# An attention block and a feed-forward block in one kernel: from a scheduler's order over four segments to a written order over eight chunks

## The chip, the core and the metric

The kernel runs on one core of a Trainium2 chip. The core has TensorE (PE: matrix products, written to PSUM), VectorE (DVE), ScalarE (ACT: exponentials, gelu, copies), GpSimd (POOL) and SyncE (SP, which here only issues transfers). The metric is device time in microseconds (us) of one execution. Each engine works through its own list of instructions in order and waits on semaphores for the others. In the profile "PEld" is the loading of the stationary operand of a product.

## The reference

Inputs are bf16; x is 2048 tokens of 576 numbers, with 32 heads of 18 numbers each.

```python
h  = x + A(layernorm(x))          # attention
h2 = h + B(layernorm(h))          # feed-forward

def A(x):                          # 4 segments of 512 tokens, M = z = 0
    q, k, v = x @ wq, x @ wk, x @ wv                 # 32 heads of 18
    for s in range(4):
        p     = softmax(q_s k_s^T * 18**-0.5, causal mask)
        a_dot = p @ v_s
        a_mem = (phi(q_s) @ M) / (phi(q_s) @ z + 1e-6)   # phi(t) = t+1 if t>0 else exp(t)
        o     = g * a_mem + (1 - g) * a_dot              # g = sigmoid(beta), per head
        M    += phi(k_s)^T v_s ;  z += sum(phi(k_s))
    return o @ wo
def B(x):
    return gelu(x @ w1 + b1) @ w2 + b2                   # 576 -> 4608 -> 576
```

The attention works inside a segment of 512 tokens; from one segment to the next only M and z go on. The feed-forward block works on each token alone.

## The kernel before, in words

Work is cut by segment of 512 tokens, four tiles of 128 tokens each. `phase_P(s)` (L218) projects: for each tile it takes the layernorm, turns it (L195), multiplies by wq, wk and wv in two halves of 288 columns (`proj`, L203 and L205), copies q and k into padded tiles (L72), turns them per group of four heads (L259, L264) and adds phi(k)^T v to M and z (L281 to L288). `load_w` fetches these weights again in every segment.

`phase_A(s)` (L300) goes over eight groups of four heads. For each group it has three steps: keys 0 to 127; keys 128 to 255 together with 384 to 511; keys 256 to 383. A step's scores (L338) are products over 32 rows, the four heads at four positions of the array. They go to two PSUM units of two banks, two heads in each, and each unit has its own exponential (L347). POOL then masks the diagonal blocks (L349), and the products with v (L356), 19 columns wide, add into one bank `ox`. That bank is cleared by DVE (L308), also holds the memory part (L323) and is read by DVE at the end of a group (L361 to L371).

`phase_B(s)` (L378) turns the result, multiplies by wo, adds x (L392), takes the second layernorm, and turns that into `xn2T_s`. It stores h + b2 to memory (`hd`, L402).

`phase_C(s)` (L405) is the feed-forward block on 512 tokens. The first layer takes w1 in nine groups of 512 columns. A group's weights `w1g` come in by three transfers on SP's queue (L410, L413, L414) into one of two buffers, are used for four blocks of five products of 512 columns (L419, L420), and DVE copies each block to `hT` (L424). After every three groups one gelu over 6144 numbers per partition runs in place (L428). The second layer (L437) is, for each tile and half, 36 products of 288 columns, added up in one bank; DVE adds `hc` (h + b2, read back, L432) and the result is stored (L441). w2 (5.3 MB) stays on the core; it is loaded once (L169), behind the first segment's inputs.

The source calls P, A and B for all segments and then C for all, but that is not the order in which the engines work. A scheduling layer places the instructions of all engines by priority, with the scores at a higher one (L334), so that products of the feed-forward block stand between the attention's products from the second segment on.

Of the kernel before, what the change touches and what calls it, by code (L numbers as in the profile page):

```python
# [16 lines left out]
def kernel(  # L17
# [15 lines left out]
    dbg = None  # L33
    nseg_run = None
# [6 lines left out]
    L = 512  # L41
    NSEG = S // L
    TPS = L // P
# [6 lines left out]
    XW = 640  # L50
    scale = float(Dh) ** -0.5
    EPS = 1e-5
    BIG = 3.0e38
    GB = 3
    FORCE4 = False
    HIPRI = True
    GB = 3
    EVAC_ACT = 0
    XT_DVE = False
    QK_DVE = False  # L60

    def copy_xt(out, in_):
        if XT_DVE:
            nc.vector.tensor_copy(out=out, in_=in_)
        else:
            nc.scalar.copy(out=out, in_=in_)  # L66

    def copy_qk(out, in_):
        if QK_DVE:
            nc.vector.tensor_copy(out=out, in_=in_)  # L70
        else:
            nc.scalar.copy(out=out, in_=in_)  # L72
    if nseg_run is None:
        nseg_run = NSEG
# [3 lines left out]
    wpool = ctx.enter_context(tc.tile_pool(name="wpool", bufs=1))  # L78
    xpool = ctx.enter_context(tc.tile_pool(name="xpool", bufs=2))
    xtp = ctx.enter_context(tc.tile_pool(name="xtp", bufs=2))  # L80
    xn2Tp = ctx.enter_context(tc.tile_pool(name="xn2Tp", bufs=2))
    tmp1 = ctx.enter_context(tc.tile_pool(name="tmp1", bufs=1))
    alpool = ctx.enter_context(tc.tile_pool(name="alpool", bufs=1))
    ptpool = ctx.enter_context(tc.tile_pool(name="ptpool", bufs=2))
    ptpool1 = ctx.enter_context(tc.tile_pool(name="ptpool1", bufs=1))
    hpool = ctx.enter_context(tc.tile_pool(name="hpool", bufs=2))
    hbpool = ctx.enter_context(tc.tile_pool(name="hbpool", bufs=1))
# [3 lines left out]
    psS = ctx.enter_context(tc.tile_pool(name="psS", bufs=2, space=PSUM))  # L91
# [3 lines left out]
    x_pre = []  # L95
    for tl in range(TPS):
        xt = xpool.tile([P, D], BF16, tag="x", name="xt") if tl < 2 else None
        if xt is not None:
            nc.sync.dma_start(out=xt[:], in_=x[tl * P:(tl + 1) * P, :])
        x_pre.append(xt)  # L100

    def load_w(W, tag):
        wt = wpool.tile([P, KT, D], BF16, tag=tag, name="wt_" + tag)
        nc.sync.dma_start(out=wt[:, 0:4, :], in_=W[0:512, :].rearrange("(k p) n -> p k n", p=P))
        nc.sync.dma_start(out=wt[0:64, 4, :], in_=W[512:576, :])
        nc.gpsimd.memset(wt[64:KTAIL, 4, :], 0.0)
        return wt

    w_pre = {"wq": load_w(A_wq, "wq"), "wk": load_w(A_wk, "wk"), "wvo": load_w(A_wv, "wvo")}
# [3 lines left out]
    maskcol = const.tile([P, 1], F32, name="maskcol")  # L113
    nc.vector.memset(maskcol[:], 0.0)
    for i in range(4):
        nc.vector.memset(maskcol[32 * i:32 * i + Dh, :], 1.0)
# [3 lines left out]
    beta_bc = const.tile([P, H], BF16, name="beta_bc")  # L120
    nc.sync.dma_start(out=beta_bc[:], in_=A_beta.partition_broadcast(P))
    g_bc = const.tile([P, H], F32, name="g_bc")
    nc.scalar.activation(out=g_bc[:], in_=beta_bc[:], func=ACT.Sigmoid)
    omg_bc = const.tile([P, H], F32, name="omg_bc")
    nc.vector.tensor_scalar(out=omg_bc[:], in0=g_bc[:], scalar1=-1.0, scalar2=1.0, op0=ALU.mult, op1=ALU.add)
    gmzm = const.tile([P, G, Dh], F32, name="gmzm")
    for i in range(4):
        src = g_bc[32 * i:32 * i + 32, :].rearrange("p (g i) -> p g i", i=4)[:, :, i:i + 1]
        nc.vector.tensor_scalar(out=gmzm[32 * i:32 * i + 32, :, :], in0=src.to_broadcast([32, G, Dh]),
                                scalar1=maskcol[32 * i:32 * i + 32, :], scalar2=None, op0=ALU.mult)  # L130

    b2_bc = const.tile([P, D], BF16, name="b2_bc")
    nc.sync.dma_start(out=b2_bc[:], in_=B_b2.partition_broadcast(P))
    b1_row = B_b1.rearrange("(o f) -> o f", o=1)
# [6 lines left out]
    q_pads = [const.tile([P, H, 32], BF16, name=f"q_pad{j}") for j in range(2)]  # L141
    k_pads = [const.tile([P, H, 32], BF16, name=f"k_pad{j}") for j in range(2)]
    phik_pads = [const.tile([P, H, 32], BF16, name=f"phik_pad{j}") for j in range(TPS)]
    v_augs = [const.tile([P, H, Dh + 1], BF16, name=f"v_aug{j}") for j in range(TPS)]
    xn_bufs = [const.tile([P, XW], BF16, name=f"xn{j}") for j in range(2)]
    xn2_bufs = [const.tile([P, XW], BF16, name=f"xn2_{j}") for j in range(1)]
    o_nat = const.tile([P, TPS, XW], BF16, name="o_nat")
    for tx in xn_bufs:
        nc.gpsimd.memset(tx[:, D:XW], 0.0)
    for tpad in q_pads + k_pads:  # L150
        nc.gpsimd.memset(tpad[:, :, Dh:32], 0.0)
    for tpad in phik_pads:
        nc.vector.memset(tpad[:, :, Dh:32], 0.0)
    for tv in v_augs:
        nc.vector.memset(tv[:, :, Dh:Dh + 1], 1.0)
    for tx in xn2_bufs:
        nc.gpsimd.memset(tx[:, D:XW], 0.0)
        nc.gpsimd.memset(tx[:, D:D + 1], 1.0)
    nc.gpsimd.memset(o_nat[:, :, D:XW], 0.0)

    hd = tc.dram_tile([S, D], F32, name="hd")
    hT = const.tile([P, NF, L], BF16, name="hT")
    w2_sb = const.tile([P, NF, D], BF16, name="w2_sb")
    w2v = B_w2.rearrange("(f p) d -> p f d", p=P)
    late = {"x_last": None, "w2_last": None}

    def issue_w2():
        for c in range(4):
            d = nc.sync.dma_start(out=w2_sb[:, c * 9:(c + 1) * 9, :], in_=w2v[:, c * 9:(c + 1) * 9, :])  # L169
            if late["x_last"] is not None:  # L170
                tc.add_manual_dep(d.ins, late["x_last"].ins.name, SYNC_DEP, reason="bulk FFN weights after the first segment's inputs")
            late["w2_last"] = d

    def layernorm(src, xn):
        stats = small.tile([P, 2, 6], F32, tag="stats", name="stats")
        for c in range(2):
            nc.vector.bn_stats(out=stats[:, c, :], in_=src[:, c * HALF:(c + 1) * HALF])  # L177
        mv = small.tile([P, 2], F32, tag="mv", name="mv")
        nc.vector.bn_aggr(out=mv[:], in_=stats[:])
        rstd = small.tile([P, 1], F32, tag="rstd", name="rstd")  # L180
        nc.vector.tensor_scalar(out=rstd[:], in0=mv[:, 1:2], scalar1=EPS, scalar2=None, op0=ALU.add)  # L181
        nc.gpsimd.tensor_tensor(out=rstd[:], in0=rstd[:], in1=mhalf[:], op=ALU.pow)  # L182
        nc.vector.tensor_scalar(out=xn[:, 0:D], in0=src, scalar1=mv[:, 0:1], scalar2=rstd[:],  # L183
                                op0=ALU.subtract, op1=ALU.mult)

    def unit2():
        return psS.tile([P, 2, 512], F32, tag="st2", name="u2")

    def bf16v(bank_ap):
        return bank_ap.bitcast(BF16)  # L190

    def transposes5(src, bank_ap):
        pt = bf16v(bank_ap)[:, 0:KT * P].rearrange("p (k q) -> p k q", q=P)
        for k in range(KT):
            nc.tensor.transpose(out=pt[:, k, :], in_=src[:, k * P:(k + 1) * P], identity=ident[:])  # L195
        return pt

    def proj(xT_t, wt):
        u = unit2()
        for hf in range(2):  # L200
            ps = u[:, hf, :]
            for k in range(4):
                nc.tensor.matmul(out=ps[:, 0:HALF], lhsT=xT_t[:, k, :], rhs=wt[:, k, hf * HALF:(hf + 1) * HALF],  # L203
                                 start=(k == 0), stop=False)
            nc.tensor.matmul(out=ps[:, 0:HALF], lhsT=xT_t[0:KTAIL, 4, :], rhs=wt[0:KTAIL, 4, hf * HALF:(hf + 1) * HALF],  # L205
                             start=False, stop=True)
        return u

    def hview(u):
        return u[:, :, 0:HALF].rearrange("p b (h d) -> p b h d", d=Dh)  # L210

    def pad_view(tpad):
        return tpad[:, :, 0:Dh].rearrange("p (b h) d -> p b h d", b=2)

    st_P = {}
    st_B = {}

    def phase_P(s):  # L218
        if s == 0:
            wq_t, wk_t, wv_t = w_pre["wq"], w_pre["wk"], w_pre["wvo"]  # L220
        else:
            wq_t = load_w(A_wq, "wq")
            wk_t = load_w(A_wk, "wk")
            wv_t = load_w(A_wv, "wvo")
        QT_al_s = alpool.tile([P, G, L], BF16, tag="qt", name="QT_al_s")
        KT_al_s = alpool.tile([P, G, L], BF16, tag="kt", name="KT_al_s")
        for tl in range(TPS):
            t = s * TPS + tl
            cols = slice(tl * P, (tl + 1) * P)
            if s == 0 and x_pre[tl] is not None:  # L230
                xt = x_pre[tl]
            else:
                xt = xpool.tile([P, D], BF16, tag="x", name="xt")
                xd = nc.sync.dma_start(out=xt[:], in_=x[t * P:(t + 1) * P, :])
                if s == 0:
                    late["x_last"] = xd
                    if tl == TPS - 1:
                        issue_w2()
# [259 lines left out]
```

## Time and profile before

| | |
|---|---|
| median of 3 runs | 618.51 us (617.55 to 622.82) |
| the profiled execution: span | 618.1 us |
| busy: PE / PEld / DVE / ACT / POOL | 553.5 / 331.1 / 327.6 / 319.4 / 154.1 us |
| first product, last product | 6.2 us, 614.6 us |
| first scores (L338), first product of the feed-forward block (L419) | 42.3 us, 119.7 us |
| TensorE's granted clock | half from about 47.9 to 123 us, full after that |
| transfers | 54.65 MB, 87 GB/s read and written over the span |
| gelu | 12 calls of 5.32 us; 17 loads of function tables of 1.28 us on ACT |

The profiled execution's own time is its span, 618.1 us, with nothing left out around it. PE's busy time is made of products that overlap one another, so what a product costs is read from the distance between the starts of two that follow each other, not from its own length.

### The profile page before, as it was taken

Reading aid. Unit: us, or ns where it says so; the run is one execution under the profiler, and the core shown is the slowest. Engines: PE = TensorE matmul, PEld = TensorE weight load, DVE = VectorE, ACT = ScalarE, POOL = GpSimd, SP = SyncE. Lnnn points to the kernel's source line nnn. Section 1 sums busy time; section 2 is a strip of 40 time slices with the busy share of each in tenths; the row PEclk is TensorE's granted clock in tenths of the full one; section 3 lists DMA queues with packets and bytes.
Section 4 is the critical chain, followed back from the end, with each engine's and each line's share of the span. In section 5 each row is a group of like instructions: output and inputs, shape, how many; then the busy total and the mean of one; then the engine's idle time right before and its main releaser. Section 6 shows DMA issues by size and latency. Waiting matters only on the chain. (4 is left out here: it accounts for less than half of the span.)

```text
span 618.1 us, 12146 instructions
## 1 busy us (share of the span) xinstructions
PE 553.5 (90%) x4992; PEld 331.1 (54%) x4992; DVE 327.6 (53%) x811; ACT 319.4 (52%) x342; POOL 154.1 (25%) x247
## 2 busy tenths in 40 slices
PE   2778875599999998999999998899999999999997
PEld 1553333375444566675444466665544567744576
DVE  5443223467777635647786735555687641166310
ACT  1449951134999931338788742368767540024300
POOL 3124432313342223224323123135331210000000
PEclk9995555599999999999999999999999999999999
DMA  7960003325223113322132333111124432144020
GB/s 194 351 201 3 2 1 97 110 65 147 65 79 110 45 59 123 104 75 85 43 89 67 114 117 117 58 45 30 31 78 116 109 123 77 38 135 129 25 58 20
DMA packets 48223, 54.65 MB, mean 88 GB/s; under 512 B 3204, under 2 KB 44072, under 8 KB 48168
## 3 DMA queue, kind: packets, MB, share of 16 engines
q1 hardware_dynamic: 48168, 53.88, 29.3%
q8 instruction: 39, 0.64, 0.4%
q14 instruction: 16, 0.13, 0.1%
HBM read 46.79 MB, written 7.08 MB: 87 GB/s over the span
## 5 line engine op out<-in xcount | busy, mean ns | idle before, releaser
L437 PEld LDWEIGHTS <-hT 128*128 128x128 bf16 x1152 | 107.5, 98 | 30.3 <-issue 3.5
L428 ACT ACTIVATE hT<-hT 128x6144 bf16<-128x6144 bf16 x12 | 63.9, 5324 | 55.8 <-DVE hT L424 55.7
L419 PEld LDWEIGHTS <-w1g 128*128 128x128 bf16 x576 | 51.3, 98 | 56.0 <-issue 7.4
L203 PEld LDWEIGHTS <-xnT_t 128*128 128x128 bf16 x384 | 36.7, 100 | 24.3 <-ACT xnT_t L66 13.4
L338 PEld LDWEIGHTS <-KT_al_s 32*128 32x128 bf16 x512 | 21.0, 93 | 50.9 <-issue 47.9
L401 POOL TENSOR_TENSOR hb<-h_t,b_bc 128x576 f32<-128x576 f32 x16 | 20.4, 1277 | 76.2 <-DVE h_t L392 76.2
L182 POOL TENSOR_TENSOR rstd<-rstd,mhalf 128x1 f32<-128x1 f32 x32 | 17.5, 549 | 40.3 <-DVE rstd L181 40.3
L314 POOL TENSOR_SCALAR r_g<-QT_al_s 128x512 bf16<-128x512 bf16 x24 | 14.7, 612 | 36.1 <-DVE pq L316 33.4
L420 PEld LDWEIGHTS <-w1g 65*128 65x128 bf16 x144 | 14.0, 97 | 14.4 <-issue 0.6
L312 ACT ACTIVATE e_g<-QT_al_s 128x512 bf16<-128x512 bf16 x24 | 15.1, 630 | 11.4 <-DVE pq L316 8.0
L203 PEld LDWEIGHTS <-oT_t 128*128 128x128 bf16 x128 | 13.6, 109 | 11.0 <-issue 4.2
L316 DVE SCALAR_TENSOR_TENSOR pq<-e_g,r_g 128x512 bf16<-128x512 bf16 x24 | 19.2, 801 | 0.3
L195 PEld LDWEIGHTS <-xn_0_167 128*128 128x128 bf16 x80 | 5.2, 107 | 22.5 <-DVE xn_0_167 L183 21.6
L308 DVE MEMSET ox<- 128x456 f32 x32 | 14.0, 438 | 3.6 <-DVE o_nat L365 1.4
L177 DVE BATCH_NORM_STATS2 stats<-xt 128x6 f32<-128x288 bf16 x32 | 13.5, 441 | 3.9 <-DMA xt<-in_A_x_dram 3.8
L183 DVE TENSOR_SCALAR xn_0_167<-h_t,mv,rstd 128x576 bf16<-128x576 f32 x16 | 9.3, 579 | 9.9 <-POOL rstd L182 9.9
L323 PEld LDWEIGHTS <-pq 128*128 128x128 bf16 x96 | 8.1, 97 | 11.9 <-issue 5.6
L177 DVE BATCH_NORM_STATS2 stats<-h_t 128x6 f32<-128x288 f32 x32 | 13.1, 451 | 0.4
L270 POOL TENSOR_SCALAR rk<-k_pad_155 128x576 bf16<-128x576 bf16 x8 | 5.4, 678 | 28.0 <-ACT k_pad_155 L72 28.0
L205 PEld LDWEIGHTS <-xnT_t 65*128 65x128 bf16 x96 | 9.7, 101 | 2.8
L270 POOL TENSOR_SCALAR rk<-k_pad_156 128x576 bf16<-128x576 bf16 x8 | 5.3, 666 | 21.9 <-ACT k_pad_156 L72 21.2
L428 ACT ACT_TABLE_LOAD x8 | 10.3, 1283 | 0.1
(1911 smaller groups left out, 1416.8 us busy)
## 6 DMA issues: line engine op xcount, KB each, us to landing
w1g<-in_B_w_dram SPq DMA_DIRECT2D x36, 512.0 KB
w_sb<-in_B_w_dram SPq DMA_DIRECT2D x4, 1296.0 KB
hd<-hb SPq DMA_DIRECT2D x16, 288.0 KB
hc<-hd SPq DMA_DIRECT2D x16, 288.0 KB
xt<-in_A_x_dram SPq DMA_DIRECT2D x16, 144.0 KB
wt_wq<-in_A_wq_dram SPq DMA_DIRECT2D x4, 576.0 KB
wt_wk<-in_A_wk_dram SPq DMA_DIRECT2D x4, 576.0 KB
wt_wvo<-in_A_wv_dram SPq DMA_DIRECT2D x4, 576.0 KB
```

Of the source, the lines that this page charges most:

```text
L177: nc.vector.bn_stats(out=stats[:, c, :], in_=src[:, c * HALF:(c + 1) * HALF])
L182: nc.gpsimd.tensor_tensor(out=rstd[:], in0=rstd[:], in1=mhalf[:], op=ALU.pow)
L203: nc.tensor.matmul(out=ps[:, 0:HALF], lhsT=xT_t[:, k, :], rhs=wt[:, k, hf * HALF:(hf + 1) * HALF], start=(k == 0), stop=False)
L308: nc.vector.memset(ox[:, 0:456], 0.0)
L312: nc.scalar.activation(out=e_g[:], in_=QT_al_s[:, g, :], func=ACT.Exp)
L314: nc.gpsimd.tensor_scalar(out=r_g[:], in0=QT_al_s[:, g, :], scalar1=BIG, scalar2=0.0, op0=ALU.min, op1=ALU.max)
L316: nc.vector.scalar_tensor_tensor(out=pq[:], in0=e_g[:], scalar=1.0, in1=r_g[:], op0=ALU.min, op1=ALU.add)
L338: mm = nc.tensor.matmul(out=sts[i // 2][:, i % 2, off:off + n], lhsT=KT_al_s[rows, g, kt * P:(kt + 1) * P], rhs=QT_al_s[rows, g, kt * P:L] ...
L401: nc.gpsimd.tensor_tensor(out=hb[:], in0=h_t[:], in1=b2_bc[:], op=ALU.add)
L419: nc.tensor.matmul(out=ps[:], lhsT=w1g[:, k, j * P:(j + 1) * P], rhs=xn2T_s[:, k, :], start=(k == 0), stop=False)
L428: nc.scalar.activation(out=hT[:, f0:f1, :], in_=hT[:, f0:f1, :], func=ACT.Gelu_apprx_tanh)
L437: nc.tensor.matmul(out=ps[:, 0:HALF], lhsT=hT[:, f, tl * P:(tl + 1) * P], rhs=w2_sb[:, f, hf * HALF:(hf + 1) * HALF], start=(f == 0), stop ...
```

## The change

The whole body is written anew. What is computed is the same.

- The work is cut into eight chunks of 256 tokens. Five generators give out the products: the second part of the attention for even and odd tiles (`stream_B`), the scores and what follows them (`stream_A`), the projections (`stream_P`) and the feed-forward block (`stream_F`).
- The order of PE's instructions is fixed in the source. A loop holds a clock `free["PE"]` and lists of taken spans for ACT, DVE and POOL, filled with durations written in the source (`pe(...)`, `op(...)`). It always goes on with the first generator, in the order B, A, P, F, whose inputs are ready by that table. The other engines' order is still the scheduling layer's.
- Scores go to one tile of four banks, all four heads at once, with one exponential per visit: 1536 numbers per partition where a visit has 384 columns, 2048 where it has 512. There is one such tile. An even chunk has one visit for each group of heads, an odd chunk two.
- Three single banks serve all the other products. Pairs of groups share a bank `ox`.
- The projections are four products of 432 columns over q, k and v together, whose weights are loaded once and stay. wo stays as well.
- The feed-forward block works on 256 tokens: a first-layer product is 256 columns wide, two blocks share a bank, gelu runs twice for each chunk (4608 numbers each), and the first half of the next chunk's first layer may stand ahead of this chunk's second layer. `w1g` still has two buffers, and w1 is fetched once for each chunk.
- w2 comes in six parts, after the fourth group of w1 has landed.

```diff
-    for s in range(n): phase_P(s); phase_A(s); phase_B(s)
-    for s in range(n): phase_C(s)
+    w1pool = ctx.enter_context(tc.tile_pool(name="w1pool", bufs=2))
+    psS = ctx.enter_context(tc.tile_pool(name="psS", bufs=1, space=PSUM))
+    psX = ctx.enter_context(tc.tile_pool(name="psX", bufs=1, space=PSUM))
+    psC = ctx.enter_context(tc.tile_pool(name="psC", bufs=3, space=PSUM))
+    def op(eng, dur, *deps):              # earliest free span of that engine
+        at = max(deps, default=0.0) + READ
+        ...
+    def pe(dur, *deps):
+        free["PE"] = max(free["PE"], max(deps, default=0.0)) + dur
+        return free["PE"] + DRAIN - READ
+    def load_w2(after):
+        for c in range(6):
+            d = nc.sync.dma_start(out=w2_sb[:, c * 6:(c + 1) * 6, :], in_=w2v[:, c * 6:(c + 1) * 6, :])
+            tc.add_manual_dep(d.ins, after.ins.name, SYNC_DEP, reason="FFN2 weights after the first FFN1 weights")
...
+        def scores(c, g, pieces):         # in stream_A: one visit
+            st = banks4()
+            for kt in pieces:
+                ...
+                for i in range(4):
+                    nc.tensor.matmul(out=st[:, i, off:off + n], lhsT=KTs[s0 + kt // 2][rows, g, (kt % 2) * P:(kt % 2 + 1) * P],
+                                     rhs=QTs[c][rows, g, lo * P:Q], start=True, stop=True, tile_position=(32 * i, 0))
+            r = pe(0.21 + off * MM / 1000, done_P[c])
+            nc.scalar.activation(out=pt_[:, :, 0:off], in_=st[:, :, 0:off], func=ACT.Exp, scale=scale)
+            lkS.give(op("ACT", 0.18 + 4 * off * 0.00083, r))
+            ...                           # masks of the diagonal blocks on POOL
...
+            plan = [[0, 1]] if half == 0 else [[0, 1], [2, 3]]
...
+    def ffn1(c, half):
+        for jp in range(9 * half, 9 * half + 9):
+            f = 2 * jp
+            ...                           # a new w1g where f % 4 == 0: L571 to L573
+                    if c == 0 and fg == W2_AFTER:   # W2_AFTER = 3
+                        load_w2(d)
+            yield lkC, done_B[c]
+            for a in range(2):
+                mm5(ps[:, a, :], lambda r, k: w1g[r, k, fs], lambda r, k: xn2T[r, k, :])
+            nc.vector.tensor_copy(out=hT[:, f:f + 2, :], in_=ps)
+        nc.scalar.activation(out=hv, in_=hv, func=ACT.Gelu_apprx_tanh)     # 18 blocks
...
+    def stream_F():
+        for c in range(NCH):
+            yield (lambda: c in done_B), 0.0
+            if ahead < c:
+                yield from ffn1(c, 0)
+            yield from ffn1(c, 1)
+            if c + 1 < NCH and c + 1 in done_B and done_B[c + 1] <= free["PE"]:
+                yield from ffn1(c + 1, 0)
+                ahead = c + 1
+            yield from ffn2(c)
+    streams = [stream_B(0), stream_B(1), stream_A(), stream_P(), stream_F()]
+    with tc.manual_schedule(engines={mybir.EngineType.PE}):
+        ...
+            pick = next((g for g, at in live if at <= t0 + 0.02), None)
+            if pick is None:
+                pick = min(live, key=lambda e: e[1])[0]
+            waits[pick] = next(pick)
```

## The prediction

> **What bounds the kernel now.** The page's busy times come first, then the stretches by window, then the timeline of PE. Everything is set against the profiled execution's own 618.1 us; the three runs' median, 618.51, is the same within 0.1%.
>
> ```profile
> span 618.1 us, 12146 instructions
> PE 553.5 (90%) x4992; PEld 331.1 (54%) x4992; DVE 327.6 (53%) x811; ACT 319.4 (52%) x342; POOL 154.1 (25%) x247
> PEclk9995555599999999999999999999999999999999
> ```
>
> PE is the bound on average, but its clock was halved for five of forty slices. By window (length; busy of PE, PEld, DVE, ACT, POOL; clock; transfer share; GB/s), cut where the first scores, the first feed-forward product and the last attention end:
>
> ```profile
> 0.00:42.30 42.30, 23.69 (x207) 17.96 (x208) 19.85 (x58) 12.88 (x19) 10.46 (x28) 1.00 0.81 245
> 42.30:119.70 77.40, 52.66 (x564) 27.54 (x563) 25.82 (x72) 45.64 (x56) 28.44 (x43) 0.54 0.18 55
> 119.70:500.00 380.30, 364.56 (x3447) 210.83 (x3445) 245.27 (x619) 237.69 (x260) 111.59 (x172) 1.00 0.28 83
> 500.00:618.10 118.10, 112.59 (x780) 74.78 (x778) 36.71 (x64) 23.16 (x7) 3.65 (x4) 1.00 0.24 71
> ```
>
> For 120 us one segment's attention runs alone, PE at half clock. From there PE is busy 364.6 of 380.3 us and does little but its work.
>
> The price of that work is the distance between starts. In the chain of waits, 36 second-layer products take 4.41 us, so 0.1225 each at 288 columns; in the timeline five first-layer products take 1.085, so 0.217 at 512:
>
> ```profile
> 516.88 4.41 PE ps_f_7058 L437 x36
> ```
>
>  The line through both gives 0.109 at 256 and 0.183 at 432. Transposes of 128 columns start 0.055 apart, products of 19 columns 0.025, of 76 columns 0.034. Scores change the array's shape, and pay for that (PE's timeline: start, length, idle before):
>
> ```profile
> 296.84 0.39 PE L338 MATMUL u_3439<-QT_al_s,KT_al_s 32*128 32x512 bf16 x2
> 297.16 0.21 PE L323 MATMUL ox<-MZ_blk_149,pq 128*128 128x76 bf16 x1
> 297.30 0.39 PE L338 MATMUL u_3440<-QT_al_s,KT_al_s 32*128 32x512 bf16 x2
> ```
>
> Two heads occupy PE for 0.32 up to the next product, and the step back costs 0.10 ahead of them (0.14 less 0.034): 0.42, where 512 columns alone are 0.21. So 0.21 is the toll of each entry. A group's six entries are 2 x (0.42 + 0.41 + 0.31) = 2.29.
>
> PE's work before is then: first layer 720 x 0.217 = 156; second 1152 x 0.1225 = 141; projections and wo 640 x 0.1225 = 78; transposes 496 x 0.055 = 27; memory 192 x 0.034 = 7; values 1280 x 0.025 = 32; scores 32 x 2.29 = 73. Sum 514. Of 618, 104 us are start, half clock and waits.
>
> **The change part by part, counted in the order of the changed program.**
>
> *PE's work.* First layer 1440 x 0.109 = 157, second 141, projections 320 x 0.183 = 58, wo 20, transposes, memory and values as before 66. Scores are 96 visits with four heads at once, one toll each: 64 of 384 columns at 0.37, 32 of 512 at 0.425: 37. **Sum 480**, 34 less.
>
> *Start.* PE has 9.7 us of work ahead of its first score visit. Before, four tiles' projections ended at 42.3 us, the first began at 12.7 behind a wait of ACT for beta (9.8 us). Two tiles by that pace: 27.5; beta's transfer is now the first of all, on POOL's queue, and wk's two are issued by ACT, which then waits anyway: 24 to 28, I take 26. **+16.**
>
> *Visits 1 to 24* (chunks 0 and 1). With one score tile, the next scores wait for the exponential. ACT's 1024 numbers take 1.02, 512 take 0.60, so 1536 are 1.44 and 2048 are 1.86; with the scores and 0.35 for two handovers, a cycle is 2.16 or 2.63. Adding per visit the larger of this cycle, PE's work up to the next visit and ACT's work gives 69 us, PE's own being 54: **+15**. PE's list is in order, so feed-forward products behind a late visit wait too.
>
> *Visits 25 to 96.* The same sum is 290 against 277 (a gelu of 4608 numbers, 4.04 by the 5.32 for 6144, plus up to two table loads, taken together with its neighbour visit, whose PE work covers it): **+13**. Where chunks 4 and 6 end, no feed-forward work stands between, and the chain through v products, transposes and layernorm is bare.
>
> *w1 twice as often.* This speaks most against the change. In the feed-forward stretch before, SP issues a reload when a group ends, and PE waits for it:
>
> ```profile
> 547.62 0.38 SPq L410 DMA_DIRECT2D w1g<-in_B_w_dram  x1
> 548.04 0.52 SPq L413 DMA_DIRECT2D w1g<-in_B_w_dram  x1
> 548.60 0.44 SPq L414 DMA_DIRECT2D w1g<-in_B_b_dram  x1
> 551.85 0.55 PEld L419 LDWEIGHTS <-w1g 128*128 128x128 bf16 x4 [0.42 <-DMA w1g<-in_B_w_dram]
> 569.47 4.95 DMA w1g<-in_B_w_dram
> ```
>
> The first is from SP's timeline, the fourth from PEld's, the last from the chain of waits. A buffer's return takes 0.2 + 4.2 = 4.4 us (4.95 once). Before, the other buffer gave 20 products, 4.33 us: hidden to within 0.1. Now it gives 20 x 0.109 = 2.18, so in a stretch of first layer alone every second group waits 2.2 us. Going through the order group by group (third needs first's release plus 4.4) gives 48 us, 29 of them after the last visit: four waits for each of three stretches of 18 blocks, two in the last. I keep 29 and half of the other 19, the rest lying under visits that are late anyway: **+38** (29 to 65, the latter with 5.0 for a return).
> The Trainium skill, "DMA: Bandwidth & Descriptors", Anatomy of one DMA, gives about 2.0 us plus bytes over 436 GB/s for a transfer of the GpSimd path; for 577 KB an estimate of 3.35, and 26 in place of 48 us. This row, on SP's queue, is longer, and I go by it.
>
> *w2 late.* Its six parts follow the fourth w1 group on SP's queue; the fifth w1 group is issued behind them, and PE's list stops at it. Between 16 and 28 us transfers ran at 355 to 369 GB/s, so 5.3 MB need 15 us, with the fourth group's return and the fifth's own transfer 22; PE has about 11 us of visits there. A wait of 11; 0 to 14, I take **+9**. Loads of x, stores of hd and out stand on the same queue; each waits for DVE or POOL, and a w1 group behind it with it. I found none ahead of a group that was due.
>
> *Clock.* The row is 47.9 to 123 us at 0.50 with PE busy 52.6 of 75.1 and attention alone. Visits 1 to 17 have projections between, so half of them might be hit; all of them at half clock would cost 17: **+8** (0 to 17).
> The skill's "TensorE: Matmul & The Clock Gate", Part 1, says that the clock drops after an idle window of some 3.4 us; by that this order, without such a gap, would lose 0, but the row fell without one.
>
> *In-order waits not counted.* Before, 119.7 to 500 lost 15.7 of 380 us (4%). DVE's work grows from 328 to 356 (its instructions in the changed program, each by the row of its size), three banks serve five streams: 5% of the 330 us up to the last visit, **+16** (0 to 40).
>
> *At nothing:* the exponentials (152 against 169 us) and three more table loads (20 x 1.28 against 17) lie under PE; DVE's 60 us after the last visit lie under 140 of PE. POOL does the same 128 masks. If that cover fails it is the first rival.
>
> *End.* The last gelu covers 18 of 36 products late: 3; from the last product to the end 3.3 as now: **+6**.
>
> 480 + 16 + 15 + 13 + 38 + 9 + 8 + 16 + 6 = **601**.
>
> **Rivals.**
> 1. *VectorE bounds the mixed part: slower.* Between first and last visit DVE has 284 us of work (356 less 12 ahead and 60 after). Its share was 0.645 in the stage from 119.7 to 500, and 0.74 from 160 to 210, its densest 50 us with PE full. At 0.645 the part lasts 440 us; with 26 ahead, 140 + 29 + 3 after, 9 for w2, 3 at the end: 650. It decides from a share under 0.70. Against: PE never waited long for DVE before. For: fewer banks.
> 2. *Two reloads in flight share the transfer engines.* One keeps them 0.8 to 1.1 busy for 2.5 us; at 5.5 a return, the waits are 80, 43 of them after the last visit, by the same reckoning 43 + 18 = 61 in place of 38: 625. Returns under 5.2 keep it below 618.
> 3. *The waits overlap.* Without w2, clock and in-order terms, with 29 for w1: 480 + 16 + 15 + 13 + 29 + 6 = 559.
>
> **Numbers.** About 1% (612 to 625) can be told from no change. The forecast has 0.60, 0.10 of it within 1%; rival 1 has 0.22 (0.04 within), rival 2 has 0.06 (0.03 within), rival 3 has 0.12. Faster 0.50 + 0.12 = 0.62; same 0.17; slower 0.21. The range runs from near rival 3 to between rival 1's break-even and its 650: 564 to 638.
>
> **What would show it.** First visit near 26 us; first feed-forward product near 65, not 119.7; clock at half for under 35 us; first-layer stretches at the end with pairs of groups 6.6 us apart, PEld waiting for w1g; one wait of 5 to 12 us for w1g behind w2; some 170 us from the last visit to the end. I am wrong if PE waits more than 50 us for DVE or ACT between visits 25 and 96, or if the mixed part exceeds 410.

## Result, and the profile after

The changed kernel takes 654.37 us (median; 649.15 to 660.72) against 618.32 us in the same session: a ratio of 1.0535, 95% interval 1.0470 to 1.0601. It is slower by about 5%, where 601 us and a gain were forecast. The ratio leaves out the run of 660.72, which fell into a slower state of the chip, and so lies below the 1.058 of the two medians. The profiled execution took 649.15 us, with a span of 647.4; it is the fastest of the four, whose spans reach 659.0. First the page: span, busy time and instructions of each engine, and the granted clock in forty slices.

```profile
span 647.4 us, 13784 instructions
PE 530.8 (82%) x5808; PEld 385.8 (60%) x5808; DVE 327.5 (51%) x839; ACT 312.1 (48%) x253; POOL 152.1 (23%) x234
PEclk9978799699999998978999976999999989989999
```

PE's share fell from 90% to 82%. The one long stretch at half clock is gone, and in its place stand a dozen short ones. By window (length; busy of PE, PEld, DVE, ACT, POOL; clock; transfer share; GB/s), cut at the first score visit, the 25th and the last; the last row takes the second and third together:

```profile
0.00:34.50 34.50, 16.02 (x82) 8.38 (x83) 16.42 (x59) 6.34 (x10) 9.81 (x25) 1.00 0.51 137
34.50:127.36 92.86, 66.53 (x874) 43.85 (x874) 46.81 (x126) 53.84 (x48) 29.11 (x44) 0.82 0.33 103
127.36:470.81 343.45, 300.55 (x3613) 216.30 (x3610) 208.92 (x560) 218.45 (x183) 108.33 (x159) 0.95 0.30 95
470.81:647.40 176.59, 147.67 (x1243) 117.25 (x1242) 55.37 (x96) 33.48 (x13) 4.88 (x6) 0.98 0.38 120
34.50:470.81 436.31, 367.08 (x4484) 260.15 (x4483) 255.73 (x685) 272.29 (x230) 137.43 (x203) 0.92 0.31 97
```

Before, PE was busy 96% of the mixed stage; now it is busy 88% of visits 25 to 96 and 84% of what follows the last visit. What it waits for is in PE's own waits (us in total, times, longest):

```profile
PE fbk L236 <- DMA w1g<-in_B_w_dram: 46.4, 29, 15.0
PE bk L231 <- DVE xn__134 L224: 10.5, 1, 10.5
PE st L379 <- ACT pt L385: 8.1, 15, 1.1
PE ox L442 <- POOL pt L390: 7.9, 14, 2.0
PE bk L231 <- DVE xn L224: 6.8, 4, 1.9
PE ox L442 <- DVE ox L400: 5.8, 8, 1.3
```

First-layer products that wait for w1 lead by far. The longest wait is the one behind w2, in the timelines of PE and of SP's queue:

```profile
106.67 0.57 PE L442 MATMUL ox<-v_aug,pt 128*128 128x19 bf16 x16
122.26 1.04 PE L236 MATMUL fbk<-xn2T,w1g 128*128 128x256 bf16 x4 [15.03 <-DMA w1g<-in_B_w_dram]
```

```profile
101.69 9.81 SPq L210 DMA_DIRECT2D w_sb<-in_B_w_dram  x6
111.60 2.34 SPq L571 DMA_DIRECT2D w1g<-in_B_w_dram  x1
113.98 1.46 SPq L572 DMA_DIRECT2D w1g<-in_B_w_dram  x1
```

SP needs 9.8 us to issue w2's six parts, and 3.8 for the next w1 group's two, where 0.9 is usual. That group is usable 10.7 us after its issue began. From 105 to 119 us the transfer engines are full, as the last two numbers of this window show (busy share, GB/s):

```profile
105.00:119.00 14.00, 2.23 (x45) 1.66 (x41) 1.58 (x3) 3.77 (x3) 1.22 (x2) 0.73 1.09 359
```

TensorE's list has a first-layer product at that place, and stops for 15 us. In the tail the same pattern is small and regular. PE's timeline, then SP's:

```profile
518.17 0.27 PE L237 MATMUL fbk<-xn2T,w1g 65*128 65x256 bf16 x1
520.70 0.66 PE L236 MATMUL fbk<-xn2T,w1g 128*128 128x256 bf16 x4 [2.26 <-DMA w1g<-in_B_w_dram]
521.37 1.06 PE L236 MATMUL fbk<-xn2T,w1g 128*128 128x256 bf16 x4
```

```profile
516.58 0.41 SPq L571 DMA_DIRECT2D w1g<-in_B_w_dram  x1
524.76 0.38 SPq L571 DMA_DIRECT2D w1g<-in_B_w_dram  x1
```

From issue to use the return takes 4.12 us here (516.58 to 520.70) and 3.84 the next time. And the wait is paid twice: the products behind it run at half clock, 1.06 us for four in place of 0.60.

To add this up, each distance between the starts of two PE products was set against its price from the prediction (0.109 us at 256 columns, 0.1225 at 288, 0.183 at 432, 0.055 for a transpose, 0.034 at 76 columns, 0.025 at 19; scores 0.37 a visit of two pieces). What is over counts as half clock, up to the product's own price, where the clock was at half, and otherwise as a wait of the product that follows:

| us of the 647.4 | all | to the first visit | visits 1 to 24 | 25 to last | after it |
|---|---|---|---|---|---|
| up to the first product | 10.5 | 10.5 | | | |
| PE's own work | 471.5 | 9.6 | 50.7 | 271.1 | 140.1 |
| waits ahead of first-layer products (w1, w2) | 60.8 | | 15.3 | 19.1 | 26.4 |
| all other waits | 72.8 | 9.6 | 17.8 | 42.0 | 3.3 |
| half clock | 28.2 | 4.7 | 9.0 | 11.2 | 3.3 |
| from the last product's start on | 3.5 | | | | 3.5 |

The record of the granted clock begins at 26.2 us, and the page counts full speed ahead of it. The half clock of the start is read from the products: those of 432 columns stand 0.35 us apart up to there (12.00 to 13.41 for four) and 0.18 after.

### The profile page after: what moved, and what is told of

Its sections match the earlier page's. It is cut to its first block, busy times and chain, and to the rows that moved or that the text cites. A ratio compares the mean times of both kernels' runs of the same rounds, so it can differ in the third digit from the quotient of the medians.

```text
span 647.4 us, 13784 instructions
## 1 busy us (share of the span) xinstructions
PE 530.8 (82%) x5808; PEld 385.8 (60%) x5808; DVE 327.5 (51%) x839; ACT 312.1 (48%) x253; POOL 152.1 (23%) x234
## 4 chain that ended last, share of the span: by engine, by line
PE 50%; DMA 18%; DVE 8%; ACT 8%; issue 7%; POOL 5%; SPq 2%; ACTq 0%; POOLq 0%; DVEq 0%
PE fbk L616 19%; DMA w1g<-in_B_w_dram 15%; PE fbk L236 11%; PE bk L236 7%; ACT pt L385 6%; PE ox L442 3%; PE st L379 3%; PE fbk L237 3%; POOL pt L390 2%; PE bk L237 2%; SPq L210 1%; DMA wqkv<-in_A_wv_dram 1%; POOL h_t L547 1%; DVE xn L224 1%; POOL rstd L222 1%
## 5 line engine op out<-in xcount | busy, mean ns | idle before, releaser
L236 PE MATMUL fbk<-xn2T,w1g 128*128 128x256 bf16 x1152 | 169.3, 277 | 48.5 <-DMA w1g<-in_B_w_dram 46.4
L385 ACT ACTIVATE pt<-st 128x2048 bf16<-128x2048 f32 (+1 forms) x96 | 152.9, 1592 | 73.7 <-PE st L379 71.8
L616 PE MATMUL fbk<-w_sb,hT 128*128 128x288 bf16 x1152 | 151.8, 288 | 3.1 <-ACT hT L592 2.7
L236 PEld LDWEIGHTS <-w1g 128*128 128x128 bf16 x1152 | 107.1, 99 | 77.4 <-DMA w1g<-in_B_w_dram 56.1
L587 DVE CAST hT<-fbk 128x512 bf16<-128x512 f32 x144 | 98.9, 688 | 106.2 <-PE fbk L237 105.7
L592 ACT ACTIVATE hT<-hT 128x4608 bf16<-128x4608 bf16 x16 | 64.7, 4044 | 120.7 <-DVE hT L587 120.7
L390 POOL TENSOR_SCALAR_AFFINE_SELECT pt<-pt 128x512 bf16<-128x512 bf16 x128 | 82.4, 667 | 166.1 <-ACT pt L385 161.6
L237 PE MATMUL fbk<-xn2T,w1g 65*128 65x256 bf16 x288 | 80.5, 279 | 3.6 <-DMA w1g<-in_B_w_dram 3.6
L236 PE MATMUL bk<-wqkv,xnT_t 128*128 128x432 bf16 x224 | 62.4, 411 | 5.3 <-DVE ot L619 2.8
L442 PE MATMUL ox<-v_aug,pt 128*128 128x19 bf16 x1280 | 48.9, 173 | 13.8 <-POOL pt L390 7.9
L442 PEld LDWEIGHTS <-pt 128*128 128x128 bf16 x1280 | 43.5, 97 | 27.5 <-POOL pt L390 13.2
L379 PEld LDWEIGHTS <-KT 32*128 32x128 bf16 x768 | 13.6, 93 | 24.9 <-issue 21.4
L296 ACT CAST qk_pad<-bk 128x432 bf16<-128x432 f32 x28 | 14.5, 518 | 27.5 <-PE bk L237 27.3
```

Source lines behind the costliest of these rows:

```text
L236: nc.tensor.matmul(out=ps, lhsT=lhsT_of(slice(0, P), k), rhs=rhs_of(slice(0, P), k), start=(k == 0), stop=False)
L237: nc.tensor.matmul(out=ps, lhsT=lhsT_of(slice(0, KTAIL), 4), rhs=rhs_of(slice(0, KTAIL), 4), start=False, stop=True)
L379: nc.tensor.matmul(out=st[:, i, off:off + n], lhsT=KTs[s0 + kt // 2][rows, g, (kt % 2) * P:(kt % 2 + 1) * P], rhs=QTs[c][rows, g, lo * P:Q ...
L385: nc.scalar.activation(out=pt_[:, :, 0:off], in_=st[:, :, 0:off], func=ACT.Exp, scale=scale)
L390: nc.gpsimd.affine_select(out=pt_[:, :, o:o + P], in_=pt_[:, :, o:o + P], pattern=[[0, 4], [1, P]], compare_op=ALU.is_ge, fill=0.0, base=0 ...
L442: nc.tensor.matmul(out=o_ps[:, g % 2, qt, i, :], lhsT=pt_[:, i, blk:blk + P], rhs=v_augs[(2 * (c - c % 2) + kt) % 6][:, 4 * g + i, :], sta ...
```

## Experiments

Theory R: the reloads of w1 and the late w2 are what makes the change slow. Theory O: the written order's other waits bound the attention part, and the reload waits only stand in their place. All waits are counted as above, from each kernel's profile; ratios are to the kernel before, run on the same chip (its medians there: 621.1 to 622.7 us). Spans and waits come from one profile each, and executions of one kernel differ by some us (spans of 647.4, 650.8 and 654.5 for the changed one), so small differences between rows are not told apart.

| kernel | ratio (95% interval) | span | w1, w2 waits | other waits | half clock | first visit |
|---|---|---|---|---|---|---|
| changed kernel | 1.0535 (1.0470 to 1.0601) | 647.4 | 60.8 | 72.8 | 28.2 | 34.5 |
| e1_w1_loaded_once | 0.9446 (0.9407 to 0.9485) | 589.7 | 4.3 | 80.0 | 20.5 | 38.1 |
| e2_w2_early | 1.0274 (1.0215 to 1.0333) | 633.8 | 49.2 | 74.0 | 25.8 | 34.5 |
| e3_w1_three | 0.9746 (0.9686 to 0.9807) | 604.7 | 15.7 | 77.4 | 26.4 | 38.3 |
| e4_start_banks | 1.0472 (1.0411 to 1.0533) | 651.5 | 63.9 | 70.0 | 33.0 | 31.0 |
| e5_three_early_banks | 0.9411 (0.9387 to 0.9436) | 583.3 | 10.1 | 67.9 | 21.2 | 25.3 |
| e6_free_order | 1.0159 (1.0079 to 1.0238) | 632.5 | 49.6 | 68.8 | 27.0 | 34.5 |
| e7_table_return | 1.0432 (1.0374 to 1.0490) | 644.9 | 57.1 | 79.4 | 24.5 | 37.7 |
| e8_no_masks | 0.9540 (0.9517 to 0.9563) | 592.9 | 17.7 | 70.1 | 21.4 | 34.4 |
| e9_filler | 0.9744 (0.9694 to 0.9795) | 606.1 | 8.4 | 46.8 | 12.8 | 24.4 |
| e10_three_free | 0.9153 (0.9112 to 0.9193) | 568.5 | 11.8 | 57.6 | 14.0 | 25.0 |
| e11_gelu_once | 0.9600 (0.9549 to 0.9651) | 598.2 | 9.6 | 78.1 | 25.9 | 25.2 |
| e12_table_handover | 0.9570 (0.9542 to 0.9599) | 596.8 | 9.7 | 74.4 | 26.7 | 24.9 |
| e13_pick_early | 0.9553 (0.9520 to 0.9585) | 594.0 | 9.1 | 80.3 | 20.0 | 24.9 |

One difference between these rows belongs to no edit. The first visit comes at about 38 us in e1, e3 and e7, and at 34.5 in the changed kernel, e2, e6 and e8. The second tile's projections ran at full speed in the changed kernel, and still at half speed in e3. PE's timelines, changed kernel first:

```profile
26.70 0.90 PE L236 MATMUL st<-wqkv,xnT_t 128*128 128x432 bf16 x4 [0.78 <-ACT xnT_t L271]
```

```profile
26.80 1.62 PE L236 MATMUL st<-wqkv,xnT_t 128*128 128x432 bf16 x4 [0.78 <-ACT xnT_t L271]
```

e8 has e3's buffers, leaves out only masks, of which none stands ahead of the first visit, and has the full speed there (0.90). So this is a matter of when the clock rose in that execution. In the rows of e1, e3 and e7 some 4 us of this half clock stand among the other waits.

**e1_w1_loaded_once**

```
-                if (c, fg) not in w1_tiles:
+                if (c, fg) not in w1_tiles and len(w1_tiles) >= 2:
+                    w1_tiles[(c, fg)] = w1_tiles[(0, fg % 2)]
+                elif (c, fg) not in w1_tiles:
...
-    W2_AFTER = 3
+    W2_AFTER = 1
```

> Part left out: only the first two groups of w1 are loaded, and every later group of 512 columns uses one of these two; w2 follows them at once. All waits of TensorE for w1 and w2 are gone, and nothing else is changed. In the changed kernel's profile the gaps ahead of first-layer products, beyond their own 0.109 us each, add up to 60 us: 15.2 in the one wait behind w2, 19 up to the last score visit, 26 after it. Theory R (reloads): this is time that nothing else would take, and the half clock around it goes too, so about 647 less 60 less 5 is 582, in any case under 597. Theory O (the written order): the attention chain is late anyway, and the 34 us up to the last visit turn into waits for the exponential and the masks; only the 26 after the last visit are gained: about 621. Between 597 and 610 both have a part.

Measured: a span of 589.7, 58 less. The waits ahead of first-layer products fell by 56 us; all others rose by 7, some 4 of them by the clock of the start (above). Theory R holds and theory O falls: time that PE spent waiting for w1 was not time in which attention was late anyway. Rid of the reloads, with their traffic, and of the late w2, the kernel is 5.5% faster than before.

**e2_w2_early**: the last edit of e1 alone.

> w2's six parts follow the second w1 group in place of the fourth. Theory R: the wait of 15.2 us at 107 us goes, about 632 us in the profile, 15 less than the changed kernel. Theory O: visits 1 to 24 are late behind their exponentials and masks, so the products that waited for w1 move into that cover only in part: 3 to 7 us less. Against both: w2's 15 us of transfers would now lie ahead of the x rows of the second chunk, and if these set the end of visit 12, nothing is gained.

Measured: 13.6 us less in the profile. The waits for w1 and w2 fell by 11.6, the half clock by 2.4, and nothing took their place. Theory R.

**e3_w1_three**

```
-    ptpool = ... (name="ptpool", bufs=3)
+    ptpool = ... (name="ptpool", bufs=2)
-    w1pool = ... (name="w1pool", bufs=2)
+    w1pool = ... (name="w1pool", bufs=3)
-    outpool = ... (name="outpool", bufs=2)
+    outpool = ... (name="outpool", bufs=1)
```

> Three w1 buffers in place of two (the room comes from one pt buffer and one output buffer). While one group returns in 4.4 us, two others hold 40 products, 4.36 us. Theory R with the transfer time of the trace before: the 45 us of waits for w1 without that for w2 fall under 8, so 35 to 40 less than the changed kernel: 607 to 612. Rival S (two returns in flight share the transfer engines, 5.5 us or more): a wait of over 1.1 us for every third group, 144 reloads less those hidden, so the gain is under 22: 625 or more. Theory O: 26 after the last visit are gained and next to nothing before it: 621.

Measured: 604.7, and 42.7 less than the changed kernel, more than theory R asked for, though its start lost 4 us to the clock; nothing in it is left out, and it beats the kernel before by 2.5% (1.9 to 3.1). (72 groups are fetched, not 144 as written above.) Its waits of PE for w1, of which 7.6 us are the one behind w2:

```profile
PE fbk L236 <- DMA w1g<-in_B_w_dram: 9.7, 7, 7.6
```

Two returns may thus be in flight without a lasting wait, and rival S falls, the prediction's second rival with it. The third pt buffer had no use: a visit's values stand in the list ahead of the scores of the next visit but one.

**e4_start_banks**

```
-                wide = c == 0
+                wide = False
```

> The first chunk's projections take single PSUM banks like the other chunks', in place of one tile of four banks. In the changed kernel each of its products waits for the copy of the one before out of the same tile: 0.61 to 0.83 us, seven times, and 2.60 once behind layernorm statistics on VectorE. Theory R takes the first visit at 34.5 as set by this: it comes at 29 or earlier, and the total falls by 4 to 6 us. Rival: the x rows and the statistics on VectorE set it, and the first visit stays above 32, the total within 2 us.

Measured: the first visit at 31.0, between the two expectations; the profiled total was no shorter (651.5), the ratio 0.6 points lower with overlapping intervals, so what it does for the total is not settled. PE's timeline of the start, changed kernel first:

```profile
12.00 1.62 PE L236 MATMUL st<-wqkv,xnT_t 128*128 128x432 bf16 x4 [0.78 <-ACT xnT_t L271]
...
14.59 1.60 PE L236 MATMUL st<-wqkv,xnT_t 128*128 128x432 bf16 x4 [0.61 <-ACT qk_pad L296]
...
21.72 1.60 PE L236 MATMUL st<-wqkv,xnT_t 128*128 128x432 bf16 x4 [2.60 <-DVE v_aug L300]
```

```profile
11.71 1.62 PE L236 MATMUL bk<-wqkv,xnT_t 128*128 128x432 bf16 x4 [0.78 <-ACT xnT_t L271]
13.12 0.57 PE L237 MATMUL bk<-wqkv,xnT_t 65*128 65x432 bf16 x1
13.48 1.65 PE L236 MATMUL bk<-wqkv,xnT_t 128*128 128x432 bf16 x4
...
21.74 1.03 PE L315 MATMUL bk<-ident,qk_pad 128*128 128x128 bf16 x8 [2.90 <-DVE v_aug L300]
```

In one tile of four banks a product waits until the copy out of another bank is done (0.61 us); in single banks it follows at once. A wait of 2.9 us stays: in DVE's order the statistics of the second chunk's rows stand ahead of the copies of v, and these rows come late, behind two w1 groups on SP's queue (DVE idles 7.2 us for them).

**e5_three_early_banks**: e3, e2 and e4 together, and one more:

```
+                    if c == 0 and fg < 3:
+                        for w in (w0, w0b, d):     # the group's three transfers
+                            tc.add_manual_dep(w.ins, x_p[3].ins.name, SYNC_DEP, ...)
```

> Four edits together: three w1 buffers as in e3_w1_three, w2 behind the second w1 group, single banks for the first chunk's projections, and the first w1 groups behind the x rows of the second chunk. If the costs found so far add: e3_w1_three's 604.7 in the profile, less 8 for the wait behind w2 that it still has, less 7 to 9 for the start (first visit at 38.3 there, at 31.0 with single banks, 30 expected): 588 to 590. Rival: the half clock (26 us in e3_w1_three) takes back part of what the start gives, since the projections run earlier but still alone: 594 to 600.

Measured: a span of 583.3, 5 us better than the sum. These 5 us are the start's: the first visit came at 25.3, which is the 26 of the prediction, and so 13 us ahead of e3's in place of 8, with e3's slow clock there gone as well. The costs add, and the rival falls: the half clock shrank too.

**e6_free_order**

```
-    with tc.manual_schedule(engines={mybir.EngineType.PE}):
+    with ExitStack():
```

> The changed kernel with the order of TensorE's instructions left to the framework's scheduler in place of the written one; w1, w2, chunks, visits and gelu halves are as changed. Theory O (the written order is what holds TensorE up, some 60 us of waits ahead of scores, values, transposes and projections): 610 to 635. Theory R (the waits come from the reloads and from a chain that any order has): no gain, and the written order is the better by what its table knows of handovers: 650 to 690.

Measured: 632.5, so theory O's range; the written order costs 15 us in the profile, and 3.8 points, some 23 us, by the ratios. But it isn't the waits it named: the others fell by 4 us only, those for w1 and w2 by 11. SP's queue is as blocked as before (9.6 us for w2's parts, from 90.92). The scheduler's list has attention visits there, and PE waits only when they are through; PE's timeline:

```profile
102.78 0.51 PE L379 MATMUL st<-QT,KT 32*128 32x256 bf16 x8 [0.36 <-ACT pt L385]
...
107.06 0.51 PE L379 MATMUL st<-QT,KT 32*128 32x256 bf16 x8 [0.56 <-ACT pt L385]
...
111.39 0.82 PE L236 MATMUL fbk<-xn2T,w1g 128*128 128x256 bf16 x3 [2.76 <-DMA w1g<-in_B_w_dram]
```

**e7_table_return**

```
+                    w1_use.append(0.0)
+                    w1_at[(c, fg)] = w1_use[-1 - W1B] + 4.4 if len(w1_use) > W1B else 0.0
...
-            yield lkC, done_B[c]
+            yield lkC, max(done_B[c], w1_at[(c, f // 4)])
...
-                r = pe(0.548, done_B[c])
+                r = pe(0.548, done_B[c], w1_at[(c, f // 4)])
+                w1_use[-1] = r
```

> The changed kernel with one thing more in the table behind the written order: a w1 buffer comes back 4.4 us after its last product, and no first-layer product is put ahead of that. Buffers and transfers are as changed. The 26 us of waits after the last visit have nothing to be filled with and stay. Theory O (the order fails because its table has no price for the return): the 19 us ahead of first-layer products between visits 25 and the last fall under 8 and the total by 9 to 14 us. Theory R (the work that is put in their place is then missing later): the total falls by less than 4 us.

Measured: 2.5 us less in the profile, with a first visit 3.2 us later by the clock of the start; by the ratios 1.0 point less, some 6 us, with intervals that overlap. Between visits 25 and the last the w1 waits fell only from 19.1 to 15.4, not under 8, so theory O's gain did not come: knowing the return helps little. Whether the total falls by less than theory R's 4 us is not settled.

**e8_no_masks**: e3 without the `affine_select` of line 390.

> Part left out: the causal masks of the probabilities on GpSimd (128 instructions of 0.67 us); TensorE's order and the three w1 buffers are those of e3_w1_three, with which it is compared. There 20 us are lost ahead of the products with the values. Theory M (the mask is the last link of the chain from scores to values): 12 to 18 us less than e3_w1_three. Rival: the exponential is late, and the mask lies under the next visit: 0 to 5 us less.

Measured: 592.9, and 11.8 less than e3. But 4.0 of these are the start's clock (first visit at 34.4 against 38.3), so behind the first visit it is some 8, between theory M and its rival. Waits ahead of the values halved (19.8 to 10.1 us), and part of them came back ahead of the scores (15.1 to 21.9): the chain of exponential, mask and values is on the path, at some 8 us for the masks.

**e9_filler** (on e5)

```
                 pick, t1 = min(live, key=lambda e: e[1])
+                if live_ox and live_ox[1] <= t0 and t1 - t0 > 0.2:
+                    for _ in range(int(0.7 * (t1 - t0) / 0.055)):
+                        nc.tensor.matmul(out=live_ox[0][:, 384:512], lhsT=ident[:], rhs=ident[:], start=True, stop=True)
```

> Base is e5_three_early_banks (583.3 in the profile). Wherever the table behind the written order foresees a wait of TensorE over 0.2 us, products of the identity with itself fill seven tenths of it, 0.055 us each, into a part of the value bank that nothing reads (941 products, 52 us of work). Theory C (the clock is halved because TensorE idles in the attention chain): the 21 us that the half clock costs in e5_three_early_banks fall under 8, and the total by 8 to 15 us, to 568 to 575. Rival: the fillers stand in order ahead of work that was ready earlier than the table thought, and the half clock comes anyway: 583 to 610.

Measured: 606.1, 23 more. The fillers, 51.8 us of them, took the place of 23 us of waits and 8 of half clock, and the rest is added time. The clock part of theory C holds in direction (half-clock cost 21.2 to 12.8, not under 8), its gain does not come. By these sums more than half of the fillers stand where PE did not really wait, so the table misjudges where the waits are.

**e10_three_free**: e5 with e6's edit.

> e5_three_early_banks with TensorE's order left to the framework's scheduler. e6_free_order lost 49 us ahead of first-layer products to w1 and 60 to all other waits, against 61 and 73 in the changed kernel. Theory R (with w1 at hand the two orders differ only in waits of the attention chain): 575 to 590, within 1.5% of e5_three_early_banks. Rival (the written order holds products back that the scheduler would put in earlier): under 575.

Measured: 570.11 us (median), 8.5% faster than before, the best of all. That is the rival's case, under 575; theory R asked for 575 or more. By window, e10 up to its first, 25th and last visit and the end, then e5 in the same cuts:

```profile
24.98:89.07 64.09, 56.54 (x808) 37.07 (x808) 45.05 (x127) 48.44 (x45) 28.46 (x43) 0.92 0.43 134
89.07:419.03 329.96, 301.57 (x3678) 219.94 (x3678) 209.06 (x563) 222.76 (x185) 110.25 (x161) 0.96 0.34 101
419.03:568.50 149.47, 142.84 (x1243) 116.16 (x1242) 54.87 (x96) 33.48 (x13) 4.87 (x6) 1.00 0.46 137
```

```profile
25.27:102.02 76.75, 65.67 (x876) 43.27 (x876) 47.27 (x131) 52.95 (x48) 29.73 (x45) 0.84 0.39 121
102.02:430.10 328.08, 296.12 (x3615) 216.56 (x3613) 208.13 (x560) 219.26 (x183) 109.26 (x159) 0.96 0.32 99
430.10:583.30 153.20, 143.72 (x1243) 116.97 (x1242) 55.11 (x96) 33.49 (x13) 4.88 (x6) 0.99 0.43 134
```

Half of the 15 us lie in visits 1 to 24, where beyond PE's own work (48.9 against 53.3 us) e10 loses 15.2 and e5 23.4 us; about 5 of these 8 us are half clock (0.92 against 0.84 in the rows). PE's order there differs in grain: the written order keeps five products of a projection and a visit's twelve value products together, the scheduler splits them (one projection product between eight and four value products, for instance) and brings scores earlier.

**e11_gelu_once** (on e5)

```
-        hv = hT[:, GB * half:GB * half + GB, :]
-        nc.scalar.activation(out=hv, in_=hv, func=ACT.Gelu_apprx_tanh)
...
+        if half == 1:
+            nc.scalar.activation(out=hT[:], in_=hT[:], func=ACT.Gelu_apprx_tanh)
```

> e5_three_early_banks with one gelu call for a chunk (9216 numbers, some 8 us by the 4.04 for 4608) after all its 36 blocks in place of two calls. Theory G (the halves are what lets the second layer begin early): second-layer products wait 4 us more at the end and in those chunks where nothing stands between: 590 to 600. Rival: other work lies under it nearly everywhere, only the last chunk pays its 4 us: 585 to 589.

Measured: 598.2, 15 more than e5: theory G. PE waits 12.9 us for gelu (8.8 at once at the end) in place of 2.7. The two calls are a part of the change that pays.

**e12_table_handover** and **e13_pick_early** (each on e5)

```
-    READ = 0.10
-    DRAIN = 0.30
+    READ = 0.25
+    DRAIN = 0.45
```

```
-            pick = next((g for g, at in live if at <= t0 + 0.02), None)
+            pick = next((g for g, at in live if at <= t0 + 0.30), None)
```

> e5_three_early_banks with the table's two handover times longer: 0.25 in place of 0.10 us before an engine starts on another's result, 0.45 in place of 0.30 from TensorE's last product to its reader. In e5_three_early_banks scores start 20 us later in sum than the table plans. Theory H (the list reaches work too early): longer handovers let the order put feed-forward work there, 570 to 579. Rival: the waits are where nothing else is at hand, and the order only moves: 582 to 592.

> e5_three_early_banks with attention work taken ahead of feed-forward work when it is ready within 0.30 us in place of 0.02. Theory P (blocks of 0.55 us of feed-forward work hold the attention chain back): 572 to 580, with the last visit before 422 in place of 430. Rival: the 0.3 us waits add up, some 100 of them at 0.1 to 0.2: 588 to 600.

Measured: 596.8 and 594.0, both some 12 us slower than e5: e13 is its rival's case, e12 is worse than even its rival's 592. Longer handover times and a wider threshold of choice, as set here, are not what the written order lacks. That the finer grain is the cause of e10's lead was seen in its order and not tested; it stays open.

## Why the prediction was wrong

The sum fell short by 46 us (601 against 647.4, the fastest run's span), and no single term did it.

- *PE's work, 480*: 471.5. Right, 8.5 too high.
- *Start, first visit at 26*: 34.5. "Two tiles by that pace: 27.5" took the pace of the kernel before, whose projections went to several units of two banks, with their rows at hand. The four-bank tile and the second chunk's rows behind two w1 groups were not in it, nor that PE would stay at half speed up to 26.2 us (4.7 of it); e5, with both mended, has 25.3 and a clock at full from 16.5. **8.5 short.**
- *w1, +38*: 45.5 (60.8 less 15.3). The tail was right: 26.4 against 29. The failing step is "half of the other 19, the rest lying under visits that are late anyway": all 19.1 came true. In a list in order, a wait for w1 ahead of a late visit moves the visit, and it isn't covered by it; e1 and e2 show that hardly anything takes its place. **7.5 short.**
- *w2, +9 (0 to 14)*: 15.3, above the bound. The reckoning gave 11: 22 us from the fourth group's issue to the fifth's use, less 11 of PE's work; 9 was taken. Measured were 24.4 (97.88 to 122.26) less the 9.3 that PE still had. So the mechanism was right, transfers at full rate with the list stopped behind them, and three sizes were off by some 2 us each: the transfers, PE's work at hand, and 9 taken for 11. **6 short.** SP's 9.8 us of issuing lie beside these transfers, and no run shows that they cost anything by themselves. That the list stops there was foreseen; e6 shows that it need not.
- *Visits 1 to 24 +15, 25 to 96 +13, in-order waits +16*: together 44, measured 59.8 (17.8 and 42.0). The in-order term came from the 4% lost in the mixed stage of the kernel before; here the waits other than w1's are 12% of the 343 us of visits 25 to 96. Masks, taken as lying under PE at nothing, cost some 8 of it (e8). What sets the rest was not tested. The first feed-forward product came at 87.0 us, not near 65. **16 short.**
- *Clock, +8 (0 to 17)*: 23.5 besides the 4.7 of the start. I looked for it in visits 1 to 17 alone. It came in every stretch with a few short waits, w1's and those at the ends of chunks 4 and 6 included. "Clock at half for under 35 us" was wrong: its pieces add up to some 75 us, as long as the single stretch of before. The sentence that this order has no idle window of 3.4 us went against the sum's own wait for w2; behind that one the clock was at half from 111.5 to 125.2. **15.5 short.**
- *End, +6*: 3.3 and 3.5. Right.

Rival 1 named 650 and the profiled time is 649, but not by its mechanism: VectorE's share from the first to the last visit is 0.59 (255.7 of 436.3), under the 0.645 it asked for, and VectorE did 327.5 us of work, not 356. Apart from the start's 10.5, PE's larger waits for it come to 19 us. "Mixed part over 410" was the sign that came true (436).

Rival 2's long returns did not come: the two shown took 4.1 and 3.8 us from issue to use, near the 4.2 of before, and wherever PE waited by more than 0.3 us they took 3.5 to 5.0 (but for the one behind w2). The estimate of 3.35 us that was worked out from the Trainium skill's "DMA: Bandwidth & Descriptors", Anatomy of one DMA, stays below all of them. Rival 3, that the waits overlap, falls with e1 and e2.

A stretch of the kernel before was misread as well: its attention runs alone for 77 us (42.3 to 119.7) and the clock is at half for 75, not for 120.

## What to carry to other kernels

Halving the columns per weight load halves the time that the other buffers cover: ask for (buffers less one) times a group's work to exceed the return, here 2 x 2.18 against some 4.1, before anything else; a third buffer was worth 43 us, and its room came from one output buffer and from a pt buffer that the order had no use for. An order fixed in the source has to hold every transfer that its list can stop at, and a sum of waits should not be discounted because "something else is late there". Price a wait with the slower clock behind it.

## What the runs showed of the hardware

The granted clock changes on a grid of 3.41 us (the pieces at half are 3.4, 6.8, 10.2, 13.7, 17.1 and in the kernel before 75.1 us long, but for each run's last, cut off at its end). I cut the traces of all fifteen kernels on that grid and took the share of each window in which PE is busy. From full clock, the next window was at half in 57 of 59 cases where PE was busy under 45%, in 87 of 329 between 45% and 75%, and in none of 1896 above. From half clock it stayed at half in all 88 cases under 80%, and went back to full in 143 of 150 at 85% or more. In the changed kernel the last window ahead of a drop was busy 30% to 59%, except behind w2, with a longest idle gap of 0.5 to 2.4 us. The Trainium skill, "TensorE: Matmul & The Clock Gate", Part 1, speaks of an idle window of some 3.4 us; only the drop behind w2 had one. The 75 us of the kernel before fit only in part. At half clock PE was busy 70% of them, and the windows from 85 to 119 us have 28% to 77%, under what brings the clock back. But those from 58.2, 68.4 and 78.7 us, with attention alone, were busy 94% to 97% and stayed at half, three of the seven exceptions above. So the share of busy time in one window is not the whole rule, and what is missing stays open. Ends of products are modelled in the trace, so these shares hold for the trace's own busy time.
